# Two Fourier layers and two dense layers on one core: half-chunk start, six W1 slots, DMA transposes, roots on ScalarE

## The chip, the cores and the metric

One core of a Trainium2 chip. The metric is the device time of one execution in microseconds (us), median of several runs. The four runs of the kernel before lie within 0.14% of each other. Each run is listed as fast or slow, by its time against the fastest of the same kernel and by its clock. A difference of 2% counts as faster or slower, less as the same; below that the 95% interval of the ratio says whether anything moved.

The engines go by short names: PE is TensorE (matmuls), DVE is VectorE, ACT is ScalarE, POOL is GpSimd and SP is SyncE; SP, ACT and POOL also issue DMAs; those that one of them issues are called its queue. The granted clock is the share of its full speed that PE was given: 1.00 is full, 0.50 is half. The DMA share is the mean busy share of the core's 16 DMA engines.

## The reference, cut to what matters

```python
# x: (1, 2048, 1024) bf16; A_w_r, A_w_i: (2048, 513); B_w1: (1024, 3584); B_b1: (3584); B_w2: (3584, 1024)
def _layernorm(x, axis=-1, eps=1e-5):
    m = jnp.mean(x, axis=axis, keepdims=True)
    v = jnp.var(x, axis=axis, keepdims=True)
    return (x - m) / jnp.sqrt(v + eps)
def _A_ref(x, w_r, w_i):                       # filter in frequency space
    X = rfft2(x.astype(jnp.float32)) * (w_r + 1j * w_i)
    return irfft2(X, s=(S, D)).astype(jnp.bfloat16)
def _B_ref(x, w1, b1, w2):                     # dense, Mish, dense
    h = x @ w1 + b1
    return (h * jnp.tanh(softplus(h))) @ w2
x = x + _A_ref(_layernorm(x), ...);  x = x + _B_ref(_layernorm(x), ...)
x = x + _A_ref(_layernorm(x), ...);  x = x + _B_ref(_layernorm(x), ...)
```

## The kernel before

The 2048 tokens are 16 tiles of 128, or four chunks of four tiles. Everything but the activations `XS` and small tables lives in one large SBUF tile, `ARENA`, cut up by hand with byte offsets. Layer A ends by turning its result through a DRAM scratch (`u_scratch`), from where it comes back into `ARENA` in runs of 256 bytes. `i4` then does the last step of layer A for a group of columns and adds it to `XS`.

```python
sb("PAD0", [64])
self.XS = sb("XS", [16, self.D])
# ...
self.RS = sb("RS", [4, 16], F32)
sb("PAD1", [96])                               # bf16: 192 bytes
# ...
self.ARENA = es.enter_context(nc.sbuf_tensor("ARENA", [P, self.arena_bytes // 2], BF))
```

Inverse roots of the variances are made on DVE by small operations (`scales`: a bit trick and two Newton steps), and the dense layer works in these steps:

```python
# transition from layer A: chunk 0 whole, then chunk 1
for u in range(4):
    self.i4(0, 4, 32 * u, 32, 2 * u)
for c in range(2):
    # ... statistics of four tiles, scales, apply, and for c == 0 four transposes by PE
# first matmuls: chunk 0 two steps ahead of chunk 1; i4 of chunks 2 and 3 and W2 loads in between
for fg in range(14 + 2):
    if fg < 14:
        mm1(0, fg)
    # ... at fg == 1: transposes of chunk 1
    if fg >= 2:
        mm1(1, fg - 2)
        while nb < min(16, 4 * (fg - 1)):
            self.i4(8, 8, 8 * nb, 8, 3 + nb % 3)
            nb += 1
    for _ in range(2):
        if w2_order and (w2_order[0] >= 16 or nb == 16):
            load_w2(w2_order.pop(0))
# second matmuls of chunks 0 and 1, with the transposes of chunks 2 and 3 by PE
for t in range(8):
    mm2(t // 4, t % 4, 0)
    transposed(2 + t // 4, t % 4, xn[8 + t])
    if t < 4:
        xn[12 + t] = self.apply(dve, 12 + t)
    mm2(t // 4, t % 4, 1)
for fg in range(14):
    mm1(2, fg)
    mm1(3, fg)
# ... mm2 of chunks 2 and 3; normalized tiles go to DRAM from SP's queue for the next layer A
```

## Time and profile before

| what | value |
|---|---|
| time, median of 4 runs | 1066.83 us (1066.41 to 1067.92) |
| PE busy | 967.1 of 1065.6 us (91%) |
| PE waits for the two DMA turns of layer A | 12.0 us each |
| PE waits for the return of the last tile into the second layer A | 11.0 us |
| second-matmul stage of chunks 0 and 1 | 100.3 us per layer |

"Busy" counts the time in which an engine has an instruction under way; the lists of waits say what ended each idle stretch.

### The profile page before, as it was taken

How to read it: one execution, taken by the hardware profiler on the slowest of the kernel's cores; microseconds unless marked ns; L12 is line 12 of the kernel's file. 1: busy time of each engine (PE TensorE's matmuls, PEld its weight loads, DVE VectorE, ACT ScalarE, POOL GpSimd, SP SyncE). 2: the span in 40 equal slices, each digit the busy share in tenths (PEclk: the TensorE clock that was granted, in tenths of full speed). 3: DMA queues.
4: the chain of work that ended last, by engine and by line, in shares of the span. 5: the costliest groups of instructions: out<-in, count | busy, mean ns of one | idle time of the engine just before them, and what ended most of it. 6: DMA issues, size and time to landing. Idle time of an engine off the chain costs nothing. (4 is left out here: it accounts for less than half of the span.)

```text
span 1065.6 us, 14051 instructions
## 1 busy us (share of the span) xinstructions
PE 967.1 (91%) x5995; PEld 510.3 (48%) x6089; DVE 360.9 (34%) x809; ACT 332.6 (31%) x468; POOL 55.4 (5%) x86
## 2 busy tenths in 40 slices
PE   0799569999999999999968965999999999999998
PEld 0678445444444444444427754444444444444443
DVE  7877482600444200034436867461012110000111
ACT  6898353342000234300007854333300014331000
POOL 2042000000000000001310200000000000000000
PEclk9699779999999999999998986999999999999999
DMA  9678732443000122211720785234500012210000
GB/s 294 147 231 271 197 101 87 151 155 122 20 20 21 56 68 75 79 60 35 146 47 29 225 205 140 70 128 158 158 21 21 20 39 69 72 40 11 20 20 30
DMA packets 138958, 102.80 MB, mean 96 GB/s; under 512 B 59952, under 2 KB 117552, under 8 KB 138896
## 3 DMA queue, kind: packets, MB, share of 16 engines
q1 hardware_dynamic: 127952, 77.29, 24.8%
q0 software_dynamic: 7856, 22.94, 7.6%
q10 hardware_dynamic: 3088, 1.67, 0.6%
q8 instruction: 48, 0.79, 0.3%
q14 instruction: 14, 0.11, 0.0%
HBM read 80.85 MB, written 20.71 MB: 95 GB/s over the span
## 5 line engine op out<-in xcount | busy, mean ns | idle before, releaser
L930 PE MATMUL PS<-ARENA 128*128 128x512 bf16 x1752 | 388.2, 381 | 4.4 <-DVE ARENA L917 2.4
L948 PE MATMUL PS<-ARENA 128*128 128x512 bf16 x1754 | 387.4, 379 | 2.0
L934 ACT ACTIVATE ARENA<-PS,B 128x512 bf16<-128x512 f32 x224 | 153.9, 687 | 438.9 <-PE PS L930 438.8
L930 PEld LDWEIGHTS PS<-ARENA 128*128 128x128 bf16 x1792 | 175.5, 98 | 213.4 <-issue 4.8
L948 PEld LDWEIGHTS PS<-ARENA 128*128 128x128 bf16 x1792 | 174.7, 98 | 207.6
L953 DVE TENSOR_TENSOR XS<-PS,XS 128x512 bf16<-128x512 f32 x64 | 44.3, 692 | 565.5 <-PE PS L948 565.5
L436 DVE BATCH_NORM_STATS2 BN<-XS 128x6 f32<-128x512 bf16 x108 | 69.5, 674 | 7.5 <-DMA XS<-in_A_x_dram 6.3
L881 DVE TENSOR_TENSOR XS<-PS,XS 128x512 bf16<-128x512 f32 (+1 forms) x40 | 29.1, 791 | 74.0 <-PE PS L875 74.0
L875 PE MATMUL PS<-MT,ARENA 128*128 128x32 bf16 (+1 forms) x768 | 24.6, 188 | 32.1 <-DMA ARENA<-u_scratch 23.9
L575 ACT ACTIVATE ARENA<-PS 128x1024 bf16<-128x1024 f32 x16 | 16.2, 1019 | 110.8 <-PE PS L569 110.5
L875 PEld LDWEIGHTS PS<-MT,ARENA 128*128 128x128 bf16 x768 | 23.0, 101 | 35.6 <-issue 27.1
L650 PE MATMUL PS<-FD,ARENA 128*128 128x256 bf16 (+1 forms) x312 | 34.5, 262 | 2.4 <-DVE ARENA L577 2.4
L695 ACT ACTIVATE ARENA<-PS 128x1024 bf16<-128x1024 f32 x32 | 33.0, 1032 | 9.0 <-PE PS L691 9.0
L417 ACT ACTIVATE ARENA<-XS 128x1024 bf16<-128x1024 bf16 x20 | 21.1, 1057 | 42.5 <-DVE XS L881 31.5
L724 ACT ACTIVATE ARENA<-PS 128x1024 bf16<-128x1024 f32 x32 | 33.0, 1030 | 3.7 <-PE PS L717 3.7
L717 PE MATMUL PS<-ARENA 128*128 128x256 bf16 x256 | 33.2, 273 | 0.1
L699 DVE TENSOR_TENSOR ARENA<-ARENA 128x1024 bf16<-128x1024 bf16 x32 | 22.1, 690 | 29.1 <-ACT ARENA L695 23.6
L650 PEld LDWEIGHTS PS<-FD,ARENA 128*128 128x128 bf16 x312 | 26.9, 101 | 7.6 <-DVE ARENA L577 2.8
L912 PE MATMUL PS<-IDENT,ARENA 128*128 128x128 bf16 x256 | 21.5, 242 | 9.2 <-DVE ARENA L479 6.7
L717 PEld LDWEIGHTS PS<-ARENA 128*128 128x128 bf16 x256 | 24.7, 98 | 9.7 <-DVE ARENA L706 0.9
L738 PE MATMUL PS<-ARENA,BD 128*128 128x256 bf16 x192 | 25.9, 273 | 0.4 <-DVE ARENA L764 0.2
L912 PEld LDWEIGHTS PS<-IDENT,ARENA 128*128 128x128 bf16 x256 | 18.6, 109 | 15.0 <-DVE ARENA L479 7.9
(66 smaller groups left out, 512.3 us busy)
## 6 DMA issues: line engine op xcount, KB each, us to landing
ARENA<-in_B_w_dram SPq DMA_DIRECT2D x56, 512.0 KB, 4.0
ARENA<-in_B_w_dram SPq DMA_DIRECT2D x56, 256.0 KB, 4.4
u_scratch<-ARENA SPq DMA_DIRECT2D x14, 512.0 KB, 3.2
ARENA<-u_scratch SPq DMA_DIRECT2D x14, 512.0 KB, 5.5
XS<-in_A_x_dram SPq DMA_DIRECT2D x4, 1024.0 KB, 8.6
ARENA<-in_A_x_dram SPq DMA_DIRECT2D x32, 128.0 KB, 3.1
w_scratch<-ARENA POOLq DMA_DIRECT2D x8, 512.0 KB, 4.9
ARENA<-w_scratch POOLq DMA_DIRECT2D x8, 512.0 KB, 3.7
```

The costliest lines, as they stand in the source:

```text
L436: self.op(self.dve, lambda e: e.bn_stats(self.BN[:, j, 6 * h:6 * h + 6], self.XS[:, j, 512 * h:512 * h + 512]), reads=[self.r_xs[j]], part ...
L650: fns.append(lambda e: e.matmul(dst, at(r), FD[:, t:t + dst.shape[-1] * 2], start=start, stop=stop))
L695: self.op(act, lambda e: e.activation(x.ap.rearrange("p a b -> p (a b)"), ps, ACT.Copy, scale=SIG), reads=banks, writes=[x.res])
L717: fns.append(lambda e, c=c, part=part: e.matmul(ps[:, c * 256:(c + 1) * 256], yk.ap[:, part, c * P:(c + 1) * P], t[:, (128, 0)[part]:(384, ...
L724: self.op(act, lambda e: e.activation(v.ap[:, :, i, :], src, ACT.Copy), reads=banks, parts=[v.res])
L875: fns.append(lambda e, l=l: e.matmul(ps[:, w * l:w * l + w], self.UT.ap[:, u0 + l, :], self.MT[:, 8 * lo:8 * lo + w], start=True, stop=True))
L881: self.op(self.dve, lambda e: e.tensor_tensor(xs, src, xs, ALU.add), reads=rb, parts=self.r_xs[lo:lo + nb])
L912: fns.append(lambda e, db=db: e.transpose(PSb[:, bank, db * P:(db + 1) * P], xn.ap[:, db * P:(db + 1) * P], self.IDENT[:]))
L930: fns.append(lambda e, db=db, bank=bank, fl=fl: e.matmul(PS[:, bank, :], wb.ap[:, db, fl * P:(fl + 1) * P], x.ap[:, db, :], start=(db == 0 ...
L934: self.op(act, lambda e, bank=bank, ft=ft: e.activation(at.ap[:, ft, :], PS[:, bank, :], ACT.Mish, bias=self.B1[:, ft:ft + 1]), reads=[sel ...
L948: fns.append(lambda e, i=i, ft=ft: e.matmul(PS[:, bank, :], at.ap[:, ft, t * P:(t + 1) * P], W2[ft].ap[:, h * 512:(h + 1) * 512], start=(i ...
L953: self.op(dve, lambda e: e.tensor_tensor(xs, PS[:, bank, :], xs, ALU.add), reads=[self.r_bank[bank]], writes=[self.r_xs[j]])
```

## The change

W1 and W2 are the two weight matrices of the dense layer; a W1 slot is a buffer for 256 columns of W1, and a step is the matmuls of one chunk with one such buffer (a numbered step is that pass of the loop over `fg`). The intent: let PE begin the dense layer on two tiles instead of four; give chunk 0 a longer lead with six W1 slots; take the transposes of chunks 2 and 3 off PE; make roots by ScalarE where they are waited for. The core of the diff:

```diff
@@ small tiles
-            sb("PAD1", [96])
+            self.EPS = sb("EPS", [2], F32)
+            sb("PAD1", [92])
@@ roots
+        self.op(self.act, lambda e: e.activation(a, var, ACT.Sqrt, bias=self.EPS[:, 0:1]), ...)
+        self.op(self.dve, lambda e: e.reciprocal(r, a), writes=rr)
@@ stores of normalized tiles
-        self.dma(self.sp, self.xn_d[j], b.ap, ...)
+        self.dma(self.pool, self.xn_d[j], b.ap, ...)
@@ W1
-        self.w1_buf = [... for i in range(4)]
+        self.w1_buf = [... for i in range(6)]
@@ transposes by DMA
+        def turned(c, t, xn):
+            for db in range(8):
+                self.dma(sp, x.ap[:, db, t * P:(t + 1) * P], xn.ap[:, db * P:(db + 1) * P], f"xt{c % 2}_{t}", ..., transpose=True)
@@ transition (cut)
+        for j in range(2):
+            self.root(j, 1)
+            xn[j] = self.apply(j)
+        ...
+        mm1(0, 0, 0)                      # 256 of 512 tokens
+        ...
+        for fg in range(4):
+            mm1(0, fg, 1)
+            if fg in (1, 3):
+                self.stats_act(6 + fg // 2)
+        self.sums_to_mv(6, 2)
+        self.scales(6, 2)
+        for j in (6, 7):
+            xn[j] = self.apply(j)
+        mm1(0, 4)
+        for j in (4, 5):
+            transposed(1, j - 4, xn[j])
+        ...
@@ first matmuls
-        for fg in range(14 + 2):
+        for fg in range(5, 14 + 3):
             if fg < 14:
                 mm1(0, fg)
-            ...
-            for _ in range(2):
+            mm1(1, fg - 3)
+            rest(3)                       # three groups of i4
+            for _ in range(3):
                 if w2_order and (...):
                     load_w2(w2_order.pop(0))
@@ second matmuls
-            transposed(2 + t // 4, t % 4, xn[8 + t])
+            if 1 <= t < 5:
+                xn[11 + t] = self.apply(11 + t)
+                turned(3, t - 1, xn[11 + t])
```

More of the change, by code (lines that the diff above doesn't have):

```diff
@@ L230, in group, with dma @@
         return t
-    def dma(self, prog, out_ap, in_ap, sem, reads=(), writes=(), parts=(), noncontig=False):
+    def dma(self, prog, out_ap, in_ap, sem, reads=(), writes=(), parts=(), noncontig=False, transpose=False):
         w = []
@@ L246, in fn @@
                     return eng.dma_start(out_ap, in_ap).then_inc(ds.sem, 16)
+            if transpose:
+                return eng.dma_start(out_ap, in_ap, transpose=True).then_inc(ds.sem, 16)
             return eng.dma_start(out_ap, in_ap).then_inc(ds.sem, 16)
@@ L336, in build @@
             self.r_ident, self.r_m, self.r_mt, self.r_fd, self.r_bd = (Res(n) for n in ("id", "m", "mt", "fd", "bd"))
-            self.r_b1 = Res("b1")
+            self.r_b1, self.r_eps, self.r_warm = Res("b1"), Res("eps"), Res("warm")
             self.r_ud = [Res(f"ud{i}") for i in range(8)]
@@ L361, in layout @@
                       FT=140 * K, BT=144 * K + 512, WT=self.W1_OFF)
-        self.ob = dict(AT0=0, AT1=36 * K, XT1=28 * K, XT0=120 * K, W2=64 * K)
+        self.ob = dict(AT0=0, AT1=36 * K, XT1=28 * K, XT0=120 * K, W2=64 * K, JUNK=54 * K)
         assert 149 * K <= self.W1_OFF, (149 * K, self.W1_OFF)
@@ L391, in prologue @@
         self.dma(sp, self.FD[:], self.con["FD"], "fd", writes=[self.r_fd])
-        self.junk = None
+        self.op(self.pool, lambda e: e.memset(self.EPS[:], 1e-5), writes=[self.r_eps, self.r_warm])
+        self.warm(ACT.Sqrt)
         self.w1_next = 0
@@ L409, in xn_ring, with warm, root @@
         self.xn_buf, self.xn_out = bufs[:4], bufs[4:]
+    def warm(self, f):
+        self.op(self.act, lambda e: e.activation(self.EPS[:, 1:2], self.EPS[:, 0:1], f), reads=[self.r_eps], writes=[self.r_warm])
+    def root(self, j0, n):
+        rr = self.r_rs[j0:j0 + n]
+        a, r = (self.RS[:, i, j0:j0 + n] for i in (1, 2))
+        var = self.MV[:, j0, 1:2] if n == 1 else self.MV[:, j0:j0 + n, 1]
+        self.op(self.act, lambda e: e.activation(a, var, ACT.Sqrt, bias=self.EPS[:, 0:1]), reads=self.r_mv[j0:j0 + n] + [self.r_eps],
+                writes=rr)
+        self.op(self.dve, lambda e: e.reciprocal(r, a), writes=rr)
     def stats_act(self, j):
@@ L447, in scales @@
         rr = self.r_rs[j0:j0 + n]
-        h, a, r, m = (self.RS[:, i, j0:j0 + n] for i in range(4))
-        mean, var = self.MV[:, j0:j0 + n, 0], self.MV[:, j0:j0 + n, 1]
+        h, a, r = (self.RS[:, i, j0:j0 + n] for i in range(3))
+        var = self.MV[:, j0:j0 + n, 1]
         def on(fn):
@@ L466, in scales, with apply @@
                 on(lambda e: e.scalar_tensor_tensor(r, a, 1.5, r, ALU.subtract, ALU.mult))
-        on(lambda e: e.scalar_tensor_tensor(m, mean, -1.0, r, ALU.mult, ALU.mult))
-    def apply(self, prog, j, out=False):
+    def apply(self, j, out=False):
         ring = self.xn_out if out else self.xn_buf
@@ L474, in apply @@
         b.unread = True
-        r, m = self.RS[:, 2, j:j + 1], self.RS[:, 3, j:j + 1]
-        if prog is self.act:
-            fn = lambda e: e.activation(b.ap, self.XS[:, j, :], ACT.Identity, scale=r, bias=m)
-        else:
-            fn = lambda e: e.tensor_scalar(b.ap, self.XS[:, j, :], r, m, op0=ALU.mult, op1=ALU.add)
-        self.op(prog, fn, reads=[self.r_xs[j], self.r_rs[j]], writes=[b.res])
+        mean, r = self.MV[:, j, 0:1], self.RS[:, 2, j:j + 1]
+        self.op(self.dve, lambda e: e.tensor_scalar(b.ap, self.XS[:, j, :], mean, r, op0=ALU.subtract, op1=ALU.mult),
+                reads=[self.r_xs[j], self.r_mv[j], self.r_rs[j]], writes=[b.res])
         return b
@@ L485, in xn_store @@
         b.unread = False
-        self.dma(self.sp, self.xn_d[j], b.ap, "xw" + b.res.name[2:], reads=[b.res], writes=[self.r_xnd[j]])
+        self.dma(self.pool, self.xn_d[j], b.ap, "xw" + b.res.name[2:], reads=[b.res], writes=[self.r_xnd[j]])
     def open_xr(self):
@@ L529, in first_scales @@
             self.sums_to_mv(j + n, 4 - n)
-        self.scales(0, 16)
+        self.root(0, 16)
         rt = self.alloc("RT", self.o["RT"], [16, 8], F32)
@@ L821, in layer_A @@
                 load_btabs(g4 + 2)
-        self.w1_buf = [self.alloc(f"W1_{i}", self.W1_OFF + i * 4096, [8, 256]) for i in range(4)]
-        while self.w1_next < 28 * li + 4:
+        self.w1_buf = [self.alloc(f"W1_{i}", (self.W1_OFF + i * 4096, 140 * K + (i - 4) * 4096)[i > 3], [8, 256]) for i in range(6)]
+        while self.w1_next < 28 * li + 6:
             self.load_w1(after=[self.UT.res])
@@ L865, in keep_filter, with i4 @@
         self.dma(self.pool, self.w_d[g], self.wt_pair(i), f"ws{g % 4}", reads=[w.res for w in self.WT[i:i + 2]], writes=[self.r_wd[g]])
-    def i4(self, lo, nb, u0, n, bank, staged=None):
+    def i4(self, lo, nb, u0, n, bank, staged=None, evac=True):
         w = 8 * nb
@@ L877, in i4, with i4_evac @@
         self.group(fns, reads=[self.UT.res, self.r_mt], writes=rb)
+        if evac:
+            self.i4_evac(lo, nb, u0, n, bank, staged)
+    def i4_evac(self, lo, nb, u0, n, bank, staged=None):
+        w = 8 * nb
+        nbank = n * w // 512
+        ps = self.PS[:, bank:bank + nbank, :].rearrange("p a b -> p (a b)")
+        rb = [self.r_bank[b] for b in range(bank, bank + nbank)]
         src = ps.rearrange("p (l c) -> p c l", c=w)
@@ L890, in load_w1 @@
         fg = n % 14
-        b = self.w1_buf[n % 4]
-        self.dma(self.sp, b.ap, self.w1.rearrange("(db dp) f -> dp db f", dp=P)[:, :, fg * 256:(fg + 1) * 256], f"w1_{n % 4}",
+        b = self.w1_buf[n % 6]
+        self.dma(self.sp, b.ap, self.w1.rearrange("(db dp) f -> dp db f", dp=P)[:, :, fg * 256:(fg + 1) * 256], f"w1_{n % 6}",
                  reads=after, writes=[b.res])
@@ L918, in transposed, with mm1 @@
             self.op(eng or dve, fn, reads=[self.r_bank[bank]], parts=[XT[c % 2].res])
-        def mm1(c, fg):
+        def turned(c, t, xn):
+            xn.unread = False
+            x = XT[c % 2]
+            if t == 0:
+                x.res.begin()
+            for db in range(8):
+                self.dma(sp, x.ap[:, db, t * P:(t + 1) * P], xn.ap[:, db * P:(db + 1) * P], f"xt{c % 2}_{t}", reads=[xn.res],
+                         parts=[x.res], transpose=True)
+        def mm1(c, fg, half=None):
             n = base + 14 * (c // 2) + fg
-            wb = self.w1_buf[n % 4]
+            wb = self.w1_buf[n % 6]
             x = XT[c % 2]
+            tok = slice(0, 512) if half is None else slice(256 * half, 256 * half + 256)
+            w = tok.stop - tok.start
             for fl in range(2):
@@ L930, in mm1 @@
                     fns.append(lambda e, db=db, bank=bank, fl=fl: e.matmul(
-                        PS[:, bank, :], wb.ap[:, db, fl * P:(fl + 1) * P], x.ap[:, db, :], start=(db == 0), stop=(db == 7)))
+                        PS[:, bank, 0:w], wb.ap[:, db, fl * P:(fl + 1) * P], x.ap[:, db, tok], start=(db == 0), stop=(db == 7)))
                 self.group(fns, reads=[wb.res, x.res], writes=[self.r_bank[bank]])
                 at, ra = AT[c % 2], r_at[c % 2][ft]
-                self.op(act, lambda e, bank=bank, ft=ft: e.activation(at.ap[:, ft, :], PS[:, bank, :], ACT.Mish,
+                self.op(act, lambda e, bank=bank, ft=ft: e.activation(at.ap[:, ft, tok], PS[:, bank, 0:w], ACT.Mish,
                                                                       bias=self.B1[:, ft:ft + 1]),
                         reads=[self.r_bank[bank], self.r_b1], writes=[ra])
-            if c % 2 and self.w1_next == n + 4 and n + 4 < base + 28:
+            if c % 2 and half != 0 and self.w1_next == n + 6 and n + 6 < base + 28:
                 self.load_w1()
@@ L961, in mm2 @@
             else:
-                self.scales(j, 1)
-                b = self.apply(dve, j, out=True)
+                if j < 14:
+                    self.scales(j, 1)
+                else:
+                    self.root(j, 1)
+                b = self.apply(j, out=True)
                 if j == 15:
@@ L977, in layer_B @@
         self.xn_ring()
-        self.junk = self.alloc("JUNK", self.o["BT"], [self.D])
+        self.junk = self.alloc("JUNK", self.ob["JUNK"], [self.D])
         YS = self.alloc("YS", self.o["YS"], [4, self.D])
@@ L983, in layer_B, with at_tiles @@
             self.r_xs[j].begin()
-        for u in range(4):
-            self.i4(0, 4, 32 * u, 32, 2 * u)
-        for c in range(2):
-            if c:
-                for j in range(4, 8):
-                    self.op(dve, lambda e, j=j: e.tensor_tensor(self.XS[:, j, :], self.XS[:, j, :], YS.ap[:, j - 4, :], ALU.add),
-                            reads=[YS.res], writes=[self.r_xs[j]])
-            for j in range(4 * c, 4 * c + 3):
-                self.stats_dve(j)
-            self.stats_act(4 * c + 3)
-            if c == 0:
-                for u in range(4):
-                    self.i4(4, 4, 32 * u, 32, 2 * (u % 3), staged=YS)
-            self.sums_to_mv(4 * c + 3, 1)
-            self.scales(4 * c, 4)
-            for t in range(4):
-                xn[4 * c + t] = self.apply(dve, 4 * c + t)
-            if c == 0:
-                for t in range(4):
-                    transposed(0, t, xn[t], dve if t % 2 else act)
-        for c in range(2):
+        def at_tiles(c):
             off = self.ob[f"AT{c}"]
@@ L1010, in layer_B, with rest @@
                 self.live.append((off + ft * 1024, off + ft * 1024 + 1024, r))
-        for j in range(8, 16):
-            self.r_xs[j].begin()
-        nb, w2_order = 0, list(range(16, 28)) + list(range(16))
-        for fg in range(14 + 2):
+        def rest(n):
+            for _ in range(n):
+                if self.nb == 0:
+                    for j in range(8, 16):
+                        self.r_xs[j].begin()
+                if self.nb < 16:
+                    self.i4(8, 8, 8 * self.nb, 8, 3 + self.nb % 3)
+                    self.nb += 1
@@ new lines, in layer_B @@
+        self.nb = 0
+        for u in range(4):
+            self.i4(0, 4, 32 * u, 32, 2 * u)
+        for u in range(3):
+            self.i4(4, 4, 32 * u, 32, 2 * u, staged=YS, evac=False)
+        self.stats_dve(0)
+        self.stats_dve(1)
+        self.stats_act(2)
+        for j in range(2):
+            self.root(j, 1)
+            xn[j] = self.apply(j)
+        self.warm(ACT.Mish)
+        for j in range(2):
+            transposed(0, j, xn[j])
+        for u in range(3):
+            self.i4_evac(4, 4, 32 * u, 32, 2 * u, staged=YS)
@@ new lines, in layer_B @@
+        at_tiles(0)
+        self.stats_dve(3)
+        self.sums_to_mv(2, 1)
+        self.scales(2, 2)
+        for j in (2, 3):
+            xn[j] = self.apply(j)
+        mm1(0, 0, 0)
+        self.i4(4, 4, 96, 32, 4, staged=YS)
+        for fg in (1, 2, 3):
+            mm1(0, fg, 0)
+        for j in (2, 3):
+            transposed(0, j, xn[j])
+        for j in range(4, 8):
+            self.op(dve, lambda e, j=j: e.tensor_tensor(self.XS[:, j, :], self.XS[:, j, :], YS.ap[:, j - 4, :], ALU.add),
+                    reads=[YS.res], writes=[self.r_xs[j]])
@@ new lines, in layer_B @@
+        self.stats_dve(4)
+        self.stats_dve(5)
+        self.scales(4, 2)
+        for j in (4, 5):
+            xn[j] = self.apply(j)
+        for fg in range(4):
[5 more added lines that the diff above has]
+        for j in (6, 7):
+            xn[j] = self.apply(j)
+        mm1(0, 4)
+        at_tiles(1)
+        for j in (4, 5):
+            transposed(1, j - 4, xn[j])
+        for fg in range(2):
+            mm1(1, fg, 0)
@@ L1017, in layer_B @@
+        for j in (6, 7):
+            transposed(1, j - 4, xn[j])
+        for fg in range(2):
+            mm1(1, fg, 1)
+        w2_order = list(range(16, 28)) + list(range(16))
+        for fg in range(5, 14 + 3):
             if fg < 14:
                 mm1(0, fg)
-            if fg == 1:
-                for t in range(4):
-                    transposed(1, t, xn[4 + t], act if t % 2 else dve)
-            if fg >= 2:
-                mm1(1, fg - 2)
-                while nb < min(16, 4 * (fg - 1)):
-                    self.i4(8, 8, 8 * nb, 8, 3 + nb % 3)
-                    nb += 1
@@ L1027, in layer_B @@
-            for _ in range(2):
-                if w2_order and (w2_order[0] >= 16 or nb == 16):
+            mm1(1, fg - 3)
+            rest(3)
+            for _ in range(3):
+                if w2_order and (w2_order[0] >= 16 or self.nb == 16):
                     load_w2(w2_order.pop(0))
@@ L1035, in layer_B @@
         for t in range(4):
-            xn[8 + t] = self.apply(dve, 8 + t)
+            xn[8 + t] = self.apply(8 + t)
+            turned(2, t, xn[8 + t])
         for t in range(8):
             mm2(t // 4, t % 4, 0)
-            transposed(2 + t // 4, t % 4, xn[8 + t])
-            if t < 4:
-                xn[12 + t] = self.apply(dve, 12 + t)
+            if 1 <= t < 5:
+                xn[11 + t] = self.apply(11 + t)
+                turned(3, t - 1, xn[11 + t])
             mm2(t // 4, t % 4, 1)
```

## The prediction

> **What bounds the kernel now.** I read first the page's table of engines (PE is busy 967.1 of 1065.6 us), then the windows view cut at the stage borders, then PE's list of waits, then the timeline at the places where PE is not fed. The windows view of the second layer (the first looks the same); the columns are the stretch, its length, busy us of PE, weight load, DVE, ACT and POOL with counts, granted clock, DMA share, GB/s:
>
> ```profile
> 631.00:643.00 12.00, 0.12 (x6) 0.04 (x2) 0.54 (x1) 1.02 (x1) 0.00 (x0) 0.60 1.04 253
> 643.00:661.00 18.00, 10.96 (x288) 10.32 (x290) 14.26 (x32) 8.00 (x10) 0.00 (x0) 0.59 0.63 177
> 661.00:673.30 12.30, 10.49 (x64) 5.26 (x65) 11.07 (x31) 6.02 (x10) 0.00 (x0) 0.88 0.00 1
> 673.30:768.70 95.40, 93.65 (x535) 44.64 (x544) 24.55 (x54) 36.03 (x52) 0.00 (x0) 1.00 0.43 138
> 768.70:869.00 100.30, 99.77 (x503) 47.42 (x512) 16.98 (x27) 0.69 (x1) 0.00 (x0) 1.00 0.07 25
> ```
>
> From 673.3 on, PE is full at clock 1.00: dense time falls only if matmuls or transposes go away. The only idle stretches that the change can touch are 643 to 673, and the end of layer B where the last tile goes back into layer A. PE's waits:
>
> ```profile
> PE PS L535 <- DVE ARENA L532: 24.4, 1, 24.4
> PE PS L875 <- DMA ARENA<-u_scratch: 23.9, 2, 12.0
> PE PS L569 <- DMA ARENA<-ARENA: 11.0, 1, 11.0
> ...
> PE PS L569 <- DMA ARENA<-in_A_x_dram: 0.9, 1, 0.9
> ```
>
> The change leaves the two 12 us DMA turns (second line) alone. The first and third lines contain a chain of small DVE operations for the root, which the change shortens. PE's timeline from the return of that DMA to the steady state:
>
> ```profile
> 642.99 5.50 PE L875 MATMUL PS<-MT,ARENA 128*128 128x32 bf16 x204 [11.88 <-DMA ARENA<-u_scratch]
> ...
> 655.86 1.89 PE L912 MATMUL PS<-IDENT,ARENA 128*128 128x128 bf16 x16 [2.76 <-DVE ARENA L479]
> 658.10 1.86 PE L912 MATMUL PS<-IDENT,ARENA 128*128 128x128 bf16 x16 [0.35 <-ACT ARENA L917]
> 661.15 8.30 PE L930 MATMUL PS<-ARENA 128*128 128x512 bf16 x31 [1.19 <-DVE ARENA L917]
> 670.17 1.08 PE L912 MATMUL PS<-IDENT,ARENA 128*128 128x128 bf16 x16 [0.72 <-DVE ARENA L479]
> 672.14 1.07 PE L912 MATMUL PS<-IDENT,ARENA 128*128 128x128 bf16 x16 [0.89 <-DVE ARENA L917]
> 673.26 6.85 PE L930 MATMUL PS<-ARENA 128*128 128x512 bf16 x31
> ```
>
> DVE in the same place (statistics of a tile, then application):
>
> ```profile
> 648.70 1.29 DVE L436 BATCH_NORM_STATS2 BN<-XS 128x6 f32<-128x512 bf16 x2
> ...
> 655.26 1.92 DVE L479 TENSOR_SCALAR ARENA<-XS,RS 128x1024 bf16<-128x1024 bf16 x4
> ```
>
> And the second-matmul stage, with the transposes that the change removes:
>
> ```profile
> 261.90 0.61 PE L912 MATMUL PS<-IDENT,ARENA 128*128 128x128 bf16 x8
> 262.35 12.25 PE L948 MATMUL PS<-ARENA 128*128 128x512 bf16 x55
> 274.44 0.61 PE L912 MATMUL PS<-IDENT,ARENA 128*128 128x128 bf16 x8
> 274.88 12.25 PE L948 MATMUL PS<-ARENA 128*128 128x512 bf16 x55
> ```
>
> The durations overlap, so read starts: eight transposes hold PE for 262.35 - 261.90 = 0.45 us, not 0.61, and 56 dense matmuls (one record is missing) for 274.44 - 262.35 = 12.09, or 0.216 us each.
>
> [...]
>
> **The change part by part.**
>
> *Chunks 2 and 3 by DMA.* Per layer 8 tiles x 0.45 = 3.6 us leave PE in a stage where it is full: -7.2 us for two layers. The cost moves to SP's DMA queue: 64 transposes per layer. In the instruction order they stand behind the last W1 loads, so they start with the second matmuls, and the stage of 448 x 0.216 = 97 us covers them if one takes under about 1.5 us in a row (97/64). [...] DVE's application of tile 12 waits for tile 8's transposes [...] but stands about 18 us into the stage. The stage runs at a DMA share of 0.07, so nothing competes.
>
> *First matmuls on half a chunk.* Durations from DVE, ACT and PE rows, for the second layer. DVE adds in until 648.7 as before. Two tiles' statistics at 1.45 us: 651.6. Roots by ScalarE behind its own statistics (they end at 650.93 now), reciprocal, two applications of 0.5: 653.1 instead of 657.2. Two transposes and two DVE copies (0.69 each): dense start near 655.3 instead of 661.15, so 5.9 us earlier. The Mish table load (1.28) ends before ScalarE's copies are needed.
>
> Then it is paid back. First pair of groups at half clock, 3.4 us; the remaining group of i4, 0.9; six groups of 256 columns at 0.87: 664.9. Tiles 2 and 3: transposes 0.9, then PE waits for the last copy, about 1.2: 666.95. Eight half groups 7.0 plus about 0.8 for ScalarE, which stops Mish for 2.2 us to sum tile 6: 674.7. One full step (3.45) and two transposes: 679.1. DVE copies these only after tiles 6 and 7, which wait for ScalarE's second sum (677.5), then 0.55 + 1.6 + 1.0 of small operations: copies end at 682.2, so PE idles 3.1 us. Four half groups, two transposes, another 1.2 us of waiting, four half groups: 691.3. By then 7 of 28 steps of 3.45 us are done. In the kernel before, 2 were done at 673.26, and the stage ended at 768.7 = 673.26 + 26 x 3.45 + 5.7, where 5.7 is four batches of i4 at 1.43. Taking three per step in place of four removes the 0.32 us bank wait of each batch: 16 x 0.28 = 4.4. So the new stage ends at 691.3 + 21 x 3.45 + 4.4 = 768.2: -0.5 per layer, -1.0 in all. The early start is nearly all spent on three new waits of PE on DVE.
>
> *Six W1 slots.* W1 is never waited for now, so slots as such give nothing; they allow chunk 0 to lead by three steps.
>
> *W2 loads.* They now begin at step 5, three at a time. W2's blocks 0 to 15 need i4 done (step 10), so the sixteenth is issued at step 15, behind a W1 load that waits for chunk 1's step 12. Only chunk 1's last step (3.45 us) follows before the second matmuls, whose first group waits for all of W2. From the DMA rows: W1's issue 0.5, then 4.3 to landing, plus the wake-up 0.1 to 0.2: 4.9 to 5.0 us. New wait 1.5 us per layer: +3.0.
>
> *Roots.* The last tile: seven DVE operations from the aggregate's end (551.45) to the application (552.95) take 1.5 us; a square root on ScalarE of some 0.3 with two hand-overs and a reciprocal of 0.16 take 0.5. This is on the chain to the 11.0 us wait: -1.0. At the kernel's start nine operations (22.20 to 24.08) shrink by 1.2 us, but PE later waits 0.9 us for the input's fourth quarter at 41.70, issued by SP until 39.04, and DVE is in order behind that: 0. The table load back to Sqrt falls where ScalarE is idle (0.69 us busy in 100).
>
> *Sum.* -7.2 - 1.0 + 3.0 - 1.0 = -6.2: 1066.5 - 6.2 = 1060.3 us.
>
> **The rivals.** (A) The DMA transpose is slow. At 2.5 us in a row, 64 are 160 us against 97: chunk 3 would be late by some 60 us per layer, and the time about 1180. For it: nothing here has measured one, and each moves only 32 KB. Against: [...] that four tiles have semaphores of their own, so one need not wait for the other. (B) The transition gains what its early start promises: no lost 3.1 us if DVE's order is kinder than I read it. Then -5 per layer in place of -0.5, and about 1051. Against: the order on DVE does put both applications before the copies. (C) The transition loses: the 3.1 us wait drops PE to half clock again, costing up to 1.7 us of each such wait; with W2 late by 2.5, the time is 1066. (D) The W2 wait is not there, since PE's queue and clock give slack: 1057.
>
> **Range and chances.** A, C and D move the sum by -3 to +6 and B by -9, so 1051 to 1069 holds it 8 times in 10. Faster by over 2% needs 1045, more than B with D: 5%. Slower needs A: 7%. Within 2%: 88%.
>
> **What would show it.** Right: no transposes between the second matmuls, that stage some 2 us shorter (100.3 to about 98.3), a first wait there of about 1.5 us on a W2 DMA; dense start 12.3 us after the return of the DMA turn (18.2 before); three waits of PE on DVE copies, one near 3 us; the last root 1 us shorter, the start unchanged. Wrong: a wait of the third or fourth chunk's first matmul on a DMA (A), or a first-matmul stage ending 3 us or more earlier (B) or later (C) than 125.7 us after the turn's return.

Half clock after the turn, which the prediction uses for the first groups, is shown: before, the clock is 0.59 from 643 to 661 and still 0.58 in the first 3.45 us of dense work, which hold 10 matmuls; in the changed kernel the first pair of groups took 3.60 us at 0.50 (predicted 3.4). The table loads on ScalarE took 1.28 us each in both kernels; the square root of the last tile took 0.29 us and its reciprocal 0.16. That a wait of 3 us would drop the clock (rival C), and its price of 1.7 us, were estimates; in layer 2 of the kernel before the first 31 dense matmuls took 8.30 us and the next 31 took 6.85, 1.45 less, and what was measured after waits of 3 us stands below.

## More of the kernel before

The columns are the transfer, queue, count, size, and the median time in us from issue to landing:

```profile
ARENA<-u_scratch SPq DMA_DIRECT2D x14, 512.0 KB, 5.5
...
ARENA<-in_A_x_dram SPq DMA_DIRECT2D x32, 128.0 KB, 3.1
```

Both write runs of 256 bytes into the large tile.

## The result

The changed kernel takes 1082.11 us (1080.62 to 1083.73, 4 runs) against 1066.83. The ratio is 1.0142, 95% interval 1.0123 to 1.0160: slower by 1.4%, inside the 2% class, but 22 us above the predicted 1060.3 and outside the range. Ratios here are the mean time of one kernel's fast runs over that of the other's of the same rounds, so not quite the ratio of the quoted medians.

The list of PE's waits of the changed kernel:

```profile
PE PS L888 <- DMA ARENA<-u_scratch: 30.5, 2, 15.3
PE PS L548 <- DVE ARENA L545: 23.2, 1, 23.2
PE PS L582 <- DMA ARENA<-ARENA: 16.4, 1, 16.4
PE PS L963 <- DVE ARENA L938: 11.0, 8, 2.9
PE PS L582 <- DMA ARENA<-in_A_x_dram: 9.5, 3, 3.5
PE PS L981 <- DMA ARENA<-in_B_w_dram: 6.6, 2, 3.6
```

Four of these six stand on a DMA. The turns, which no part of the change seemed to touch, take 15.3 us instead of 12.0. The wait for the input grew from 0.9 to 9.5 us, in the first 50 us of the kernel, where the program has hardly changed. The return of the last tile takes 16.4 instead of 11.0. The last line is the predicted wait for W2, twice the size. The rows of the DMA issues that answer to those of before:

```profile
ARENA<-u_scratch SPq DMA_DIRECT2D x14, 512.0 KB, 7.3
...
ARENA<-in_A_x_dram SPq DMA_DIRECT2D x32, 128.0 KB, 5.2
```

The same transfers of the same size take 1.8 and 2.1 us longer. The loads of `XS` from the same input, into a tile of its own, stay at 8.7 us (8.6 before).

PE's timeline in the first transition and at the start of the second matmuls:

```profile
147.43 3.60 PE L963 MATMUL PS<-ARENA 128*128 128x256 bf16 x16 [0.79 <-DVE ARENA L938]
...
159.53 6.29 PE L963 MATMUL PS<-ARENA 128*128 128x256 bf16 x56 [0.94 <-DVE ARENA L938]
...
174.59 3.67 PE L963 MATMUL PS<-ARENA 128*128 128x256 bf16 x32 [2.86 <-DVE ARENA L938]
...
180.09 10.57 PE L963 MATMUL PS<-ARENA 128*128 128x256 bf16 x63 [0.94 <-DVE ARENA L938]
...
263.06 99.77 PE L981 MATMUL PS<-ARENA 128*128 128x512 bf16 x439 [3.06 <-DMA ARENA<-in_B_w_dram]
```

The transition runs as worked out: `i4` starts at 135.46, dense work 12.0 us later (predicted 12.3), then come waits of 0.94, 2.86 and 0.94 us on DVE copies (predicted 1.2, 3.1, 1.2). The first matmuls end at 260.0, 124.5 us after the turn's return; before it was 255.86 - 130.31 = 125.55. The second matmuls lose 3.06 us to W2 and then more. The windows view (columns as in the prediction) right there:

```profile
259.00:263.00 4.00, 1.01 (x5) 0.28 (x3) 0.00 (x0) 0.69 (x2) 0.00 (x0) 0.90 1.08 308
263.00:269.00 6.00, 5.93 (x15) 2.06 (x16) 0.00 (x0) 0.00 (x0) 0.00 (x0) 0.50 0.23 52
269.00:275.00 6.00, 5.95 (x28) 2.74 (x28) 1.39 (x2) 0.00 (x0) 0.00 (x0) 1.00 0.13 27
```

While PE waits, DMA is full (share 1.08); then PE runs 6 us at clock 0.50 and does 15 matmuls where the next 6 us hold 28. That is 3 us lost on top of the wait.

The DMA transposes stayed hidden. From the view of their source line: count, duration of one on SP's queue in ns (least, median, most), first and last start:

```profile
L248 SPq DMA_TRANSPOSE ARENA<-ARENA x64: 1212/1232/2165, 260.5 to 343.6; - x64
```

64 in about 84 us, hidden under the second matmuls.

Adding up the stages by PE's milestones (start of `i4` after each turn, start of the second matmuls, start of the second layer A, end):

| milestone | before | after | shift | added in this stage |
|---|---|---|---|---|
| first turn back | 130.31 | 135.46 | +5.2 | +5.2: slower input, +1.8 up to the turn; turn +3.3 |
| second matmuls, layer 1 | 255.86 | 263.06 | +7.2 | +2.0: W2 +3.1, transition -1.0 |
| second layer A starts | 560.68 | 572.59 | +11.9 | +4.7: clock +3.0, transposes -3.6, return +5.4 |
| second turn back | 642.99 | 657.92 | +14.9 | +3.0: slower turn |
| second matmuls, layer 2 | 768.70 | 785.99 | +17.3 | +2.4: W2 +3.6, transition -1.2 |
| end | 1065.6 | 1079.4 | +13.8 | -3.5: transposes |

So what was predicted is there, and something that slows DMA everywhere has been added to it.

### The profile page after: what moved, and what is told of

Same layout as the page of the kernel before. It is cut to its first block, busy times and chain, and to the rows that moved or that the text cites. A ratio compares the mean times of both kernels' runs of the same rounds, so it can differ in the third digit from the quotient of the medians.

```text
span 1079.4 us, 14332 instructions
## 1 busy us (share of the span) xinstructions
PE 959.7 (89%) x6063; PEld 521.2 (48%) x6153; DVE 350.9 (33%) x775; ACT 339.5 (31%) x504; POOL 64.1 (6%) x102
## 5 line engine op out<-in xcount | busy, mean ns | idle before, releaser
L963 PE MATMUL PS<-ARENA 128*128 128x512 bf16 (+1 forms) x1946 | 392.4, 361 | 14.2 <-DVE ARENA L938 11.0
L981 PE MATMUL PS<-ARENA 128*128 128x512 bf16 x1756 | 388.4, 381 | 8.5 <-DMA ARENA<-in_B_w_dram 6.6
L967 ACT ACTIVATE ARENA<-PS,B 128x512 bf16<-128x512 f32 (+1 forms) x248 | 159.6, 645 | 449.8 <-PE PS L963 449.8
L963 PEld LDWEIGHTS PS<-ARENA 128*128 128x128 bf16 x1984 | 194.3, 99 | 205.4 <-DVE ARENA L938 12.6
L981 PEld LDWEIGHTS PS<-ARENA 128*128 128x128 bf16 x1792 | 175.9, 98 | 220.8 <-issue 11.5
L453 DVE BATCH_NORM_STATS2 BN<-XS 128x6 f32<-128x512 bf16 x104 | 67.2, 675 | 7.5 <-DMA XS<-in_A_x_dram 6.3
L434 ACT ACTIVATE ARENA<-XS 128x1024 bf16<-128x1024 bf16 x24 | 25.3, 1055 | 43.2 <-DVE XS L902 38.2
L708 ACT ACTIVATE ARENA<-PS 128x1024 bf16<-128x1024 f32 x32 | 33.0, 1032 | 9.1 <-PE PS L704 9.1
L737 ACT ACTIVATE ARENA<-PS 128x1024 bf16<-128x1024 f32 x32 | 33.0, 1031 | 3.7 <-PE PS L730 3.7
L249 POOL DMA_DIRECT2D xn_scratch<-ARENA x15 | 8.3, 554 | 401.5 <-DVE ARENA L492 401.5
L730 PEld LDWEIGHTS PS<-ARENA 128*128 128x128 bf16 x256 | 24.6, 98 | 9.9 <-DVE ARENA L719 0.9
L492 DVE TENSOR_SCALAR ARENA<-XS,MV,RS 128x1024 bf16<-128x1024 bf16 x48 | 25.0, 543 | 5.5 <-DMA xn_scratch<-ARENA 4.5
```

The source lines that it names most:

```text
L453: self.op(self.dve, lambda e: e.bn_stats(self.BN[:, j, 6 * h:6 * h + 6], self.XS[:, j, 512 * h:512 * h + 512]), reads=[self.r_xs[j]], part ...
L708: self.op(act, lambda e: e.activation(x.ap.rearrange("p a b -> p (a b)"), ps, ACT.Copy, scale=SIG), reads=banks, writes=[x.res])
L730: fns.append(lambda e, c=c, part=part: e.matmul(ps[:, c * 256:(c + 1) * 256], yk.ap[:, part, c * P:(c + 1) * P], t[:, (128, 0)[part]:(384, ...
L737: self.op(act, lambda e: e.activation(v.ap[:, :, i, :], src, ACT.Copy), reads=banks, parts=[v.res])
L963: fns.append(lambda e, db=db, bank=bank, fl=fl: e.matmul(PS[:, bank, 0:w], wb.ap[:, db, fl * P:(fl + 1) * P], x.ap[:, db, tok], start=(db ...
L967: self.op(act, lambda e, bank=bank, ft=ft: e.activation(at.ap[:, ft, tok], PS[:, bank, 0:w], ACT.Mish, bias=self.B1[:, ft:ft + 1]), reads= ...
```

## The experiments

Thirteen kernels ran, all with correct results, each beside runs of the kernel before on the same chip. Where no other figure is given, "before" has a median between 1066.60 and 1066.87.

### First theory: a DMA transpose in the program slows all DMAs

The new kind of DMA was the obvious suspect, though the slowing starts in the first 50 us and the first transpose at 260.46.

**e1: the kernel before and one DMA transpose.**

```diff
+        if last:
+            self.dma(sp, self.M[:], self.IDENT[:], "turn1", reads=[self.r_ident], writes=[self.r_m], transpose=True)
```

> The kernel before, plus one single DMA transpose of a 128x128 constant into an unused tile during the last second-matmul stage of the last layer, where DMA is nearly idle. Theory H1 (that a program contains a DMA transpose at all makes its ordinary DMAs with 256-byte runs slower, from the first microsecond): the time rises by about 10 us (1.8 at the start, 3.3 at each of the two DMA turns, some at the return into the second layer A), the wait of the first-stage matmuls on the input's DMA grows from 0.9 towards 9.5 us and each wait on the u_scratch turn from 12.0 to 15.3. Rival H2 (the slowing comes from something else in the change, such as stores on the POOL queue, six W1 slots or the early ScalarE and POOL instructions): same time within 0.3% and those waits as in the kernel before.

Measured: 1066.61 us, ratio 0.9998 (0.9981 to 1.0015). The stage that took the transpose has a DMA share of 0.06 in the kernel before. From its list of PE's waits:

```profile
PE PS L879 <- DMA ARENA<-u_scratch: 23.7, 2, 11.9
PE PS L573 <- DMA ARENA<-ARENA: 10.9, 1, 10.9
```

**e2: the changed kernel with all transposes by PE.** Edit: the `turned` calls out, the `transposed` calls of before back in.

> The changed kernel with chunks 2 and 3 transposed by PE as before, everything else of the change kept; no DMA transpose left in the program. H1: the waits on the DMA turns fall back to 12.0 us and the start to 0.9, so minus 8 to 10 us, plus 7.2 us of PE transposes: about 1079 to 1082, with the W2 waits of 3 us shrinking to some 1.5 to 2.5 as the W1 and W2 loads no longer lag. H2: the DMA waits stay at 15.3 and 9.5 and the time rises by the 7.2 us of transposes to about 1089.

Measured: 1089.97 us, ratio 1.0214 (1.0198 to 1.0229, across the 2% line and so unclear by class), the longer turn 15.5 us. No DMA transpose is left and the DMAs are as slow as ever; the time rises by the 7.9 us that the PE transposes cost. The first theory falls with both runs, the rival H2 (about 1089) is met, and the DMA transposes are a gain even in the slow kernel.

### Two known losses, one by one

**e3: stores from SP again.**

```diff
-        self.dma(self.pool, self.xn_d[j], b.ap, "xw" + b.res.name[2:], ...)
+        self.dma(self.sp, self.xn_d[j], b.ap, "xw" + b.res.name[2:], ...)
```

> The changed kernel with the normalized tiles stored from the SP queue again instead of POOL. Theory: in the changed kernel the last stores stand on POOL behind loads of the same queue, so the last tile's load and two of the direct rows come late (PE waits 16.4 us there, 11.0 before); undone, the wait falls to about 11 to 12 and the time by 4 to 5 us, to about 1077. Rival: the 16.4 us come from the slower 256-byte packets themselves, then the wait stays above 14 and the time falls by less than 2.

Measured: 1081.71 us, ratio 1.0133 (1.0118 to 1.0148), overlapping the changed kernel's interval. The wait did fall:

```profile
PE PS L582 <- DMA ARENA<-ARENA: 13.1, 1, 13.1
```

That is 3.3 us less than 16.4, as the theory said, and still 2 us above the kernel before. The time did not follow, a miss. In the profiled execution the second W2 wait was followed by a half-clock stretch that the changed kernel's profile had not had there (63 matmuls in the first 16.67 us after it against 64 in 14.19), but the first stage lost less, so that the two second-matmul stages differ little (97.51 and 99.76 us against 99.77 and 96.85). What is taken back stands in the two transitions: the 32 half matmuls (256 columns instead of 512) after each wait of 2.86 and 2.85 us took 5.33 us, in the changed kernel 3.67, so 3.3 us in all. That is one execution; whether it explains the medians is not shown.

**e4: W2 four blocks a step.**

```diff
-            for _ in range(3):
+            for _ in range(4):
                 if w2_order and (w2_order[0] >= 16 or self.nb == 16):
```

> The changed kernel with W2 loaded four blocks a step instead of three, so that the last is issued at step 13 and not behind the W1 load of step 15. Theory: both waits on W2 (3.1 and 3.6 us) go, and with them the stretch of some 6 us at half clock that follows each (3 us lost each): minus 12 to 13 us, to about 1069. Rival: the half clock comes from something else (the DMA transposes that start there), then only the waits go: minus 6.6, to about 1075.

Measured: 1073.76 us (1069.20 to 1074.07), ratio 1.0054 (1.0033 to 1.0074). Both W2 waits are gone. The gain is 8.3 us: the 6.6 us of waits and some of the half clock, between theory and rival. The rival's cause falls: the DMA transposes are still there, and the first second-matmul stage now runs without a half-clock stretch (96.86 us; 99.77 in the changed kernel). A stretch at half clock does not follow every wait, nor the same wait in every execution: in the changed kernel's profile it came after the first W2 wait alone (0.50 for 6 us; after the second, of 3.6 us, the first 6 us ran at 1.00), so the expectation was wrong to count it twice.

### Second theory: the working tile lost its alignment

The built program lists where each tile lies. Before, `PAD1` starts at byte 59968 and `ARENA` at 60160, which is 235 x 256. In the changed kernel `EPS`, 8 bytes long, lies at 59968, but `PAD1` at 60000 and `ARENA` at 60192: the small tile takes 32 bytes, and the padding was cut by only 8. Every offset in `ARENA` moved by 32 bytes. The buffers that the two slowed loads fill lay on 256-byte boundaries and no longer do.

**f1: the kernel before, shifted by 32 bytes.**

```diff
-            sb("PAD1", [96])
+            sb("PAD1", [112])
```

> The kernel before with nothing but 32 bytes more of padding ahead of the large working tile, so that it starts at byte 60192 as in the changed kernel and not at 60160. Theory S (the added small tile takes 32 bytes and the padding was cut by only 8, so that the working tile lost its 64-byte alignment, and DMA of 256-byte runs into it takes about a quarter longer): the waits on the u_scratch turns go from 12.0 to about 15.3 us each, the wait on the input from 0.9 to about 9, and the time rises by 10 to 12 us, to about 1077 to 1079. Rival: alignment doesn't matter, 1066.8 and the waits as before.

Measured: 1079.67 us, ratio 1.0125 (1.0110 to 1.0140). Its waits:

```profile
PE PS L875 <- DMA ARENA<-u_scratch: 30.5, 2, 15.4
PE PS L569 <- DMA ARENA<-ARENA: 14.2, 1, 14.2
PE PS L569 <- DMA ARENA<-in_A_x_dram: 11.3, 4, 3.1
```

Sixteen elements of unused padding, no instruction changed, and the kernel shows the DMA waits of the changed one. The milestones say the same: the first turn is back at 135.49 (5.2 us later than before), the second layer A starts at 569.01 (8.3 later), the second turn is back at 654.32 (11.3 later), and the end comes at 1076.9, again 11.3 later. So all that this execution lost stands at these places.

**f2: the changed kernel, aligned again.**

```diff
-            sb("PAD1", [92])
+            sb("PAD1", [80])
```

> The changed kernel with 24 bytes less padding, so that the working tile starts at 60160 again; nothing else. Theory S: the turns fall to 12.0 us each, the start to about 0.9, the time by 10 to 12 us to about 1071. Rival: unchanged at 1082.

Measured: 1063.95 us (1062.42 to 1064.73), ratio 0.9972 (0.9955 to 0.9989). Its waits:

```profile
PE PS L888 <- DMA ARENA<-u_scratch: 23.9, 2, 12.0
PE PS L582 <- DMA ARENA<-ARENA: 10.1, 1, 10.1
PE PS L582 <- DMA ARENA<-in_A_x_dram: 8.2, 3, 3.8
PE PS L981 <- DMA ARENA<-in_B_w_dram: 5.4, 2, 2.9
```

Twelve elements of padding give 18.2 us, 7 more than expected and more than the 13 that the shift costs the kernel before. Most of the surplus is visible. The return falls by 6.3 us where f1 explains 3.2: in the changed kernel POOL, whose queue the change loaded with stores, issues its rows of the last tile at 566.59, 7.5 us after SP issues its own (559.12), in the aligned one at 551.06, 0.3 us after (550.79). And the W2 waits shrink by 1.2. The input's wait did not go back to 0.9: the changed kernel reaches this place earlier (its first PE instruction is at 22.95, 24.36 before) and now waits on the DMA 8.2 us in three pieces, where the kernel before waited 5.9 us in seven small ones, six of them on DVE and ACT. The first matmuls of the next step start at 47.92, before at 47.49. That is the predicted zero of the root at the kernel's start.

**g1 and i1: shifts by 64 and 128 bytes**, with `PAD1` at 128 and 160 elements, to see which alignment counts.

> The kernel before with 64 bytes more padding: the large working tile starts at 60224, a multiple of 64 and not of 128. If what counts is the 64-byte alignment, the time stays at 1066.6 within 0.3% and the u_scratch turns at 12.0 us; if it is 128 bytes or more, they lie near the 15.3 us of the 32-byte shift and the time above 1072.

Measured: 1077.34 us, ratio 1.0096 (1.0079 to 1.0113).

> The kernel before with 128 bytes more padding, the large working tile starting at 60288, a multiple of 128 and not of 256. If 128 bytes are enough: 1066.6 within 0.3%, u_scratch turns of 12.0 us. If it takes 256, the length of one run: 1077 and 15 us, as for the 64-byte shift.

Measured: 1078.35 us, ratio 1.0112 (1.0095 to 1.0129). The turns of both, g1 first:

```profile
PE PS L875 <- DMA ARENA<-u_scratch: 29.9, 2, 15.0
```

```profile
PE PS L875 <- DMA ARENA<-u_scratch: 34.2, 2, 17.7
```

Neither 64 nor 128 bytes is enough; of four starts only the multiple of 256, the length of one run, is fast (turns of 12.0 us; 15.4, 15.0 and 17.7 with the shifts of 32, 64 and 128). The 64 bytes that theory S named were a guess, and g1 refutes it. A second multiple of 256 was not tried: upwards there is no room (the layout fits the 128-byte shift to the last byte), and downwards `XS` would have had to move as well. Buffers counted from the arena's end, the W1 slots among them, did not move with the shifts of 64 and 128, since the arena shrank by as much; so the effect does not rest on them. Before, they start at 60160 + 169088 - 4 x 4096 = 212864, which is 128 bytes off a multiple of 256, and whether they would gain from alignment was not tested.

Why such a start is slow is not shown. The DMAs are cut into as many packets: f1 moves 138,958 packets and 102.80 MB, 59,952 of the packets under 512 bytes, all as before. What grows is the time that the packets take, as a share of 16 engines' span from 24.8 to 27.4% in the largest queue (q1). Transfers that only write to the shifted tile are among the slow ones (the input's load, 3.1 to 5.2 us).

### What is left, and the best version

**f3 and f4: aligned, with W2 early; then also stores from SP.** The edits are those of f2, e4 and e3.

> As the aligned one, and W2 four blocks a step. The two faults add up: 1071 minus the 8.3 us that the same edit took off the unaligned kernel, about 1062. If the W2 waits are shorter with the faster loads, minus 5 only: 1065.

Measured: 1056.18 us, ratio 0.9903 (0.9886 to 0.9920). That is under both figures, because f2 had come out 7 us under its own; the W2 fault is worth 7.8 us in the aligned kernel. Its waits were 5.4, and the rest fits the half clock after them: from 252 to 262 us the granted clock is 0.83 in f2 and 1.00 in f3, and the two second-matmul stages take 98.25 and 98.41 us in f2, 96.86 each in f3, which is 3.0 in all.

> As the last, and the tiles stored from SP instead of POOL. Theory: POOL's order costs 3 us at the return into the second layer A in the unaligned kernel (16.4 against 13.1 us of wait); aligned, its loads are faster and the queue may keep up: between 0 and 4 us less than the last, 1058 to 1062. That would be 0.5 to 0.8% under the kernel before.

Measured: 1055.51 us, ratio 0.9896 (0.9881 to 0.9910). 0.7 us less, inside the overlap: with alignment, the queue that the stores stand on makes no difference that these runs can see.

**e6: the kernel before with only the DMA transposes.**

> The kernel before with only chunks 2 and 3 transposed by DMA from SP; nothing else of the change. Step one of the prediction: PE's second-matmul stage loses 3.6 us per layer, so 1066.6 minus 7.2: 1059.4; the stage's DMAs stay hidden. Rival: the stage loses less, since the transposes are late at first or the stores wait behind them on SP: between 1061 and 1067.

Measured: 1060.01 us, ratio 0.9936 (0.9921 to 0.9950): 6.7 us, predicted 7.2. PE's timeline of the stage:

```profile
255.03 96.86 PE L960 MATMUL PS<-ARENA 128*128 128x512 bf16 x439
351.73 18.51 PE L942 MATMUL PS<-ARENA 128*128 128x512 bf16 x83
```

351.73 - 255.03 = 96.7 us, as worked out (448 x 0.216), with no break.

**g2: f4 with the transposes by PE.**

> The aligned kernel with early W2 and SP stores (1055.5), but chunks 2 and 3 transposed by PE again: plus 7.2 us, to about 1062.7. What remains below 1066.6 is the half chunk and the roots: predicted minus 2.0 together, measured here as about minus 4.

Measured: 1064.54 us, ratio 0.9976 (0.9961 to 0.9991): 9.0 us more than f4, above the expected 7.2 and the 6.7 of e6, which is not explained, and 2.2 us below the kernel before, not 4. Half-chunk start and roots, with six slots and the early W2 that only keeps its fault away, are thus worth 2.2 us, where the prediction had 2.0.

**h1: f4 with another order on DVE.** The copies of tiles 4 and 5 go ahead of the small operations of tiles 6 and 7:

```diff
-        self.sums_to_mv(6, 2)
-        self.scales(6, 2)
-        for j in (6, 7):
-            xn[j] = self.apply(j)
         mm1(0, 4)
         at_tiles(1)
         for j in (4, 5):
             transposed(1, j - 4, xn[j])
+        self.sums_to_mv(6, 2)
+        self.scales(6, 2)
+        for j in (6, 7):
+            xn[j] = self.apply(j)
```

> The aligned kernel with early W2 and SP stores, and on DVE the two copies of tiles 4 and 5 ahead of the small operations and applications of tiles 6 and 7. The 2.85 us wait of PE in each transition should go, and in part come back as a longer wait before tiles 6 and 7 (0.94 us now, some 2 then): minus 1.5 to 2.5 us per layer, to about 1051 to 1052.5. Rival: the later wait grows by as much, no gain.

Measured: 1050.75 us (1048.63 to 1052.26), ratio 0.9847 (0.9832 to 0.9861), the best of all. PE's timeline of the first transition, in f4 where the wait of 2.85 us stands:

```profile
167.59 5.33 PE L963 MATMUL PS<-ARENA 128*128 128x256 bf16 x32 [2.85 <-DVE ARENA L938]
```

and in h1 at the same place and after it:

```profile
163.88 3.67 PE L963 MATMUL PS<-ARENA 128*128 128x256 bf16 x32 [0.94 <-DVE ARENA L938]
169.38 10.57 PE L963 MATMUL PS<-ARENA 128*128 128x256 bf16 x63 [0.94 <-DVE ARENA L938]
```

The first wait is now 0.94, and the later one did not grow (0.94 in both). That is 2 x 1.9 = 3.8 of the 4.8 us gained. The 32 half matmuls after the wait took 5.33 us in f4's first transition and 3.67 here; in f4's second transition they took 3.67 too.

## Why the prediction was wrong

**The missing term.** No step of the prediction has it. The roots' part counts the instructions of the new root and not the 32 bytes of its new constant; "The change leaves the two 12 us DMA turns (second line) alone" and, of the kernel's start, "0" are the sentences that failed. What ran instead: each turn took 3.3 us longer (12.0 to 15.3), the wait for the input grew from 0.9 to 9.5, and that for the return from 11.0 to 16.4, where 10.0 had been predicted. The shift alone costs the kernel before 13 us (f1) and the changed one 18.2 (f2). Without it the changed kernel measures 1063.95, inside the predicted range and 3.6 above its centre. The rivals did not have it either: A was about the transposes, C about half clock and W2. Nor did the range come out of its sum: A stands there with -3 to +6, though its own text puts it at about 1180, and +6 gives 1066, not 1069.

**The W2 wait, mis-sized.** The mechanism held: the sixteenth block stands behind a W1 load and PE waits for it. The term of +3.0 measured 5.4 us of waits in the aligned kernel and 7.8 in time. It used a landing of 4.3 us, from a kernel that asks for two blocks a step; with three, DMA is full at that moment (share 1.08), and the last blocks land 5.9 us after issue in the changed kernel, 5.7 in the aligned one. Put in the prediction's own sum, 0.5 + 5.7 + 0.1 - 3.45 = 2.85, and f2's first wait is 2.86. The half clock that followed stood only in rival C, as a price of other waits and at 1.7 us; after the first W2 wait of the changed kernel it was 3 us. For the wait that C meant, the one of some 3 us in the transition, its price is right where it is paid: 5.33 - 3.67 = 1.66 us, in the first transition of e4 and f4 and in both of e3, and in none of the changed kernel, f2 and f3, after a wait of 2.85 or 2.86 us in each. So the length of the wait alone does not say whether the clock drops.

**What held.** Transposes: -7.2 predicted, -6.7 alone (e6), with 1.23 us per DMA transpose on the queue and 1.32 from start to start, under the 1.5 up to which the stage covers them. Transition: its start and three waits were right to 0.3 us, its sum (-1.0 and -1.2 for -0.5) to 0.7. Root of the last tile: from the aggregate's end to the application 0.56 us instead of 1.5, and the wait for the return is 10.1 instead of 11.0 in the aligned kernel: -0.9, predicted -1.0. The root at the start: nothing, as predicted. W1 slots: PE never waited for W1. Rival B, that the transition gains 9 us more, needed another order on DVE; h1 gains 4.8 with one, so this order was indeed a part of the obstacle.

**What stays open.** Why a start off a multiple of 256 bytes is slow, why moving the stores to SP did not pay in the medians of the unaligned kernel (e3), when exactly a wait of 3 us ends in half clock, and whether reads suffer as writes do: in f1 the half of the turn that writes the shifted tile in 256-byte runs went from 5.5 to 7.2 us, the half that reads it (`u_scratch<-ARENA`, in longer runs) from 3.2 to 3.6.

## What to carry to other kernels

A change in the list of small tiles moves every tile behind it: compare the start addresses of the tiles that DMA reads and writes in short runs before and after. Here the start at a multiple of 256 bytes had turns of 12.0 us and the three others 15.0 to 17.7 (256 is also the length of a run, so the runs can't say which of the two counts). When DMAs are slower that the change never touched, look for what they share, such as an address, before suspecting the new instruction. And move work off a full engine only after checking that the loads which the new order delays still land before their first use, since a wait can cost twice its length where the clock drops: in the changed kernel one of 3.06 us was followed by 6 us at clock 0.50, which lost 3 us more.
